# Gates and values of six batches by Strassen's scheme: seven block products in place of eight

## The chip, the core and the metric

The kernel runs on one core of one Trainium2 chip. The metric is the device time of one execution in microseconds (us); lower is better. TensorE (PE) multiplies, VectorE (DVE), ScalarE (ACT) and GpSimd (POOL) work elementwise, SyncE (SP) issues all DMAs.

## The reference, cut to what matters

```
x   = attention(q, k, v)        # 8 batches x 8 heads x 576 tokens x 64: a band of
                                # +-3 keys, plus attention over means of 4 tokens
x   = x.reshape(4608, 512)      # 8 batches x 576 tokens
out = (sigmoid(x @ w_gate) * (x @ w_val)) @ w_out    # 512 -> 1536 -> 512, all float32
```

## The kernel before

A float32 product is made of f16 products: each factor is split into a high and a low f16 part, and `product` issues three matmuls (high·high, high·low, low·high) into one accumulation. The work goes batch by batch (576 tokens, in two halves of HN = 288 columns):

- **Gates and values.** The 1536 columns of w_gate and of w_val are 12 pieces of 128 (`fc`). `moe_gate` and `moe_val` multiply one piece by the batch: 2 halves x 4 row blocks j of 128 x 3 = 24 matmuls of 128x288. ACT turns a gate into tanh, DVE forms (tanh + 1)·value (line 591), ACT writes the high f16 part of that into `gq`, DVE the low part (`split`, lines 163 and 164).
- **Output.** `moe_out` makes 4 row blocks m, each 2 halves x 12 pieces x 3 = 72 matmuls, tile `po`; ACT or DVE scales it into `osb`, SP stores it.
- **Attention.** Four units (head pairs) per batch, computed during the batch before: scores `s`, `sd`, transposes `at`, `adt`, products `x`, `od`; the tile `xs` holds a unit's x, and `xsplit` makes its f16 parts in `xT`.
- **Weights.** 36 pieces of 512 KB are loaded into four staging buffers during batch 0, unpacked from 64-bit words on ACT and DVE (`wjoin`), scaled, and split into f16 (`wsplit`: DVE, ACT, then POOL at line 251). From then on they stay in SBUF.

The order of the work is the table T: each step has a position, the steps are recorded by position, and a scheduler places the instructions of each engine in a fixed order. Each engine runs its own in that order and waits on semaphores. PSUM has 8 banks: the pool `ps_m` holds 2 tiles of 2 banks (gates, values, outputs), `ps_a` holds 4 of one bank (attention).

## Time and profile before

| what | value |
|---|---|
| median of 3 runs | 1096.45 us (1092.32 to 1097.87) |
| profiled execution | 1095.66 us, its span 1093.9 us |
| PE busy | 1063.1 us, 97% of the span |
| DVE, ACT, POOL busy | 47%, 36%, 32% |
| mean granted TensorE clock | 0.983 of full speed |

The span runs from the first to the last instruction; the execution is 1.76 us longer. PE's busy share counts a matmul from start to modelled end; how fast matmuls follow each other is read from the chain of work that ended last.

### The profile page before, as it was taken

What the parts mean: (1) busy time and instruction counts of PE and PEld (TensorE: products, weight loads), DVE (VectorE), ACT (ScalarE), POOL (GpSimd) and SP (SyncE); (2) the same over time, 40 slices, a digit from 0 to 9 for tenths busy, and PEclk for the clock granted to TensorE, in tenths of its full rate; (3) what the DMA queues carried; (4) which work ended last, traced back from release to release, by engine and by line L of the source; (5) the groups of instructions that cost most, each with busy time, mean ns of one, the idle gap of its engine ahead of it and who ended that gap; (6) DMA issues with size and microseconds to landing.
All of it is one profiled execution on the core that took longest, in us unless ns stands there. A gap on an engine that the chain in (4) does not pass through costs nothing.

```text
span 1093.9 us, 23031 instructions
## 1 busy us (share of the span) xinstructions
PE 1063.1 (97%) x9935; PEld 852.5 (78%) x9935; DVE 515.7 (47%) x1010; ACT 393.4 (36%) x878; POOL 345.5 (32%) x395
## 2 busy tenths in 40 slices
PE   9787988999999999999999999999999999999998
PEld 7575666878788787878788787878888787887776
DVE  7779989355632445234641445225452445302210
ACT  4744547233431344224341334224341344302210
POOL 7332577333321343233322333223432333100000
PEclk9779999999999999999999999999999999999999
DMA  9426643422121121221212221221112220000001
GB/s 368 154 77 212 217 177 134 138 72 74 60 83 54 63 75 59 94 82 60 97 35 93 71 75 59 83 90 53 62 46 94 82 74 1 4 32 12 1 10 36
DMA packets 33078, 91.90 MB, mean 84 GB/s; under 512 B 4688, under 2 KB 10960, under 8 KB 32976
## 3 DMA queue, kind: packets, MB, share of 16 engines
q1 hardware_dynamic: 32976, 90.42, 24.2%
q8 instruction: 78, 1.28, 0.5%
q14 instruction: 24, 0.20, 0.1%
HBM read 80.97 MB, written 9.44 MB: 83 GB/s over the span
## 4 chain that ended last, share of the span: by engine, by line
PE 86%; DVE 6%; POOL 2%; ACT 2%; DMA 2%; issue 1%; SPq 0%; ACTq 0%; DVEq 0%; POOLq 0%
PE po L365 25%; PE pg L365 23%; PE pv L365 23%; PE s L365 3%; PE x L365 3%; PE sd L365 2%; PE od L365 2%; PE at L508 1%; DMA wv<-in_wv_dram 1%; PE adt L518 1%; PE awake L82 1%; POOL wg L251 1%; DMA wg<-in_wg_dram 1%; DVE wv L209 1%; DVE hmx L159 1%
## 5 line engine op out<-in xcount | busy, mean ns | idle before, releaser
L365 PE MATMUL pg<-xT,wg 128*128 128x288 f16 x2304 | 304.7, 289 | 8.6 <-POOL wg L251 5.7
L365 PE MATMUL pv<-xT,wv 128*128 128x288 f16 x2304 | 301.8, 286 | 2.5 <-DVE tanh L591 2.4
L365 PE MATMUL po<-gq,wo 128*128 128x288 f16 x2304 | 289.4, 286 | 2.9 <-ACT wo L163 1.8
L365 PEld LDWEIGHTS <-wg 128*128 128x128 f16 x2304 | 224.5, 99 | 71.4 <-POOL wg L251 6.6
L365 PEld LDWEIGHTS <-wo 128*128 128x128 f16 x2304 | 223.3, 98 | 61.1 <-ACT wo L163 2.6
L365 PEld LDWEIGHTS <-wv 128*128 128x128 f16 x2304 | 224.0, 98 | 59.1 <-issue 3.1
L591 DVE SCALAR_TENSOR_TENSOR tanh<-tanh,pv 128x576 f32<-128x576 f32 x96 | 72.0, 750 | 203.3 <-PE pv L365 203.2
L163 ACT ACTIVATE gq<-tanh 128x576 f16<-128x576 f32 x96 | 65.6, 684 | 200.5 <-DVE tanh L591 199.8
L586 ACT ACTIVATE tanh<-pg,tsc 128x576 f32<-128x576 f32 x96 | 70.9, 739 | 123.7 <-PE pg L365 123.7
L164 DVE SCALAR_TENSOR_TENSOR gq<-tanh,gq 128x576 f16<-128x576 f32 x96 | 79.1, 824 | 25.9 <-ACT gq L163 25.4
L559 POOL TENSOR_TENSOR xT<-xs,xT 128x576 f16<-128x576 f32 x27 | 37.0, 1370 | 120.9 <-ACT xT L557 120.8
L606 DVE TENSOR_SCALAR osb<-po,osc 128x576 f32<-128x576 f32 (+1 forms) x16 | 12.8, 799 | 125.1 <-PE po L365 107.8
L442 POOL TENSOR_TENSOR t<-t,mx 128x640 f32<-128x640 f32 x32 | 41.5, 1297 | 82.6 <-DVE mx L441 81.9
L354 POOL TENSOR_TENSOR qkd<-qkd 128x576 f32<-128x576 f32 x29 | 36.2, 1249 | 93.4 <-DMA qkd<-in_qkd_dram 89.1
L430 DVE SCALAR_TENSOR_TENSOR t<-s,mk 128x384 f32<-128x384 f32 x64 | 30.0, 485 | 56.6 <-PE s L365 56.1
L608 ACT ACTIVATE osb<-po,osc 128x576 f32<-128x576 f32 (+1 forms) x17 | 12.3, 726 | 122.9 <-PE po L365 122.9
L452 POOL TENSOR_TENSOR t<-t,sm 128x640 f32<-128x640 f32 x26 | 33.7, 1296 | 57.0 <-DVE sm L450 46.3
L493 POOL TENSOR_TENSOR ad<-e,sme 72x288 f32<-72x288 f32 x50 | 32.8, 675 | 57.1 <-PE adt L518 38.4
L164 DVE SCALAR_TENSOR_TENSOR vblk<-v,svb,vblk 64x640 f16<-64x640 f32 x48 | 46.3, 965 | 5.1 <-ACT vblk L163 4.3
L365 PEld LDWEIGHTS s<-qk 64*64 64x64 f32 x1200 | 39.5, 134 | 11.0 <-issue 8.5
L448 DVE TENSOR_REDUCE sm<-t 128x10 f32<-128x640 f32 x32 | 26.1, 817 | 45.9 <-ACT t L443 45.9
L476 ACT ACTIVATE e<-sd,mxd 72x144 f32<-72x144 f32 x128 | 47.0, 370 | 2.0
(119 smaller groups left out, 1099.8 us busy)
## 6 DMA issues: line engine op xcount, KB each, us to landing
qk<-in_qk_dram SPq DMA_DIRECT2D x30, 610.0 KB, 4.3
qkd<-in_qkd_dram SPq DMA_DIRECT2D x29, 576.0 KB, 4.1
vd<-in_vd_dram SPq DMA_DIRECT2D x29, 384.0 KB, 4.6
v<-in_v_dram SPq DMA_DIRECT2D x32, 320.0 KB, 4.2
wg<-in_wg_dram SPq DMA_DIRECT2D x12, 512.0 KB, 3.6
wv<-in_wv_dram SPq DMA_DIRECT2D x12, 512.0 KB, 4.9
wo<-in_wo_dram SPq DMA_DIRECT2D x12, 512.0 KB, 3.7
out_dram<-osb SPq DMA_DIRECT2D x8, 256.0 KB, 2.1
```

The lines of the kernel that those rows point to most:

```text
L163: nc.scalar.activation(hi, src, AF.Copy, scale=sc)
L164: return nc.vector.scalar_tensor_tensor(out=lo, in0=src, scalar=sc, in1=hi, op0=ALU.mult, op1=ALU.subtract)
L354: nc.gpsimd.tensor_tensor(out=x[:, :, 0:2], in0=x[:, :, 0:2], in1=x[:, :, 2:4], op=ALU.add)
L365: nc.tensor.matmul(o, w[a], x[c], start=first and i == 0, stop=last and i == len(pairs) - 1)
L430: nc.vector.scalar_tensor_tensor(out=s["t"][:, j0:j1, :], in0=pt[:, : n * 2 * WIN].rearrange("p (a b) -> p a b", a=n), scalar=QKSCALE, in1 ...
L442: nc.gpsimd.tensor_tensor(out=t, in0=t, in1=mx.unsqueeze(2).to_broadcast([P, NBLK, WIN]), op=ALU.subtract)
L452: eng.tensor_tensor(out=t, in0=t, in1=sm.unsqueeze(2).to_broadcast([P, NBLK, WIN]), op=ALU.mult)
L476: nc.scalar.activation(s["e"][:, qb, h, :], pt[:QM, h * SD : (h + 1) * SD], AF.Exp, bias=mx[:, h : h + 1], scale=QKSCALE / 16, accum_out=s ...
L493: eng.tensor_tensor(out=AD[:, qb].rearrange("p c h k -> p h c k")[:, :, :, :KC], in0=s["e"][:, qb].rearrange("p h (c k) -> p h c k", c=NKC ...
L559: eng.tensor_tensor(out=x[:, hp, 1], in0=s["xs"], in1=x[:, hp, 0], op=ALU.subtract)
L586: nc.scalar.activation(t, pt, AF.Tanh, scale=tsc[:, b, fc : fc + 1])
L591: nc.vector.scalar_tensor_tensor(out=t, in0=t, scalar=1.0, in1=pt, op0=ALU.add, op1=ALU.mult)
```

## The change

For batches 2 to 7 two neighbouring pieces of a weight matrix (256 columns) are multiplied together, as 2x2 blocks: the rows of x (512) as two halves of two row blocks q, the weight columns as two pieces, the tokens as two halves. Strassen's scheme (Winograd's form) makes the four result blocks from seven products of sums of blocks in place of eight. Per batch there are 12 such pairs (`pair(b, n)`, gates and values alternating). A pair has seven products, each 2 x 3 = 6 matmuls of 128x288. ACT copies three of them out of PSUM into `sx`, POOL makes three sums in SBUF, DVE adds the other four from PSUM into the result tile. Then tanh, or (tanh + 1)·value and the split, run on 1152 columns at once.

- The sums of weight blocks are made once, during batch 1 (`sums(p, k)`, 12 of them). They go to HBM (`wd`) with the three plain blocks: seven blocks, 917 KB a pair. `wring` streams them back through three SBUF slots, one load per pair, 12 per batch.
- The sums of x blocks are made per two units (`xparts`).
- PSUM: `ps_m` has 5 tiles of one bank, `ps_a` 3; batches 0 and 1 keep the plain products, each half evicted by itself.
- Weights share one scale per pair of pieces; the tiles for weights, x and staging become parts of one arena, since the ring and the new tiles reuse their room. The positions in T differ.

```diff
-WGROUPS = [(0, 2), (2, 4), (4, 6), (6, 8), (8, 10), (10, NPC)]
+WGROUPS = [(0, 1), (1, 2), (2, 3), (3, 4), (4, 5), (5, 6)]
-    ps_m = ctx.enter_context(tc.tile_pool(name="ps_m", bufs=2, space=PSUM))
-    ps_a = ctx.enter_context(tc.tile_pool(name="ps_a", bufs=4, space=PSUM))
+    ps_m = ctx.enter_context(tc.tile_pool(name="ps_m", bufs=5, space=PSUM))
+    ps_a = ctx.enter_context(tc.tile_pool(name="ps_a", bufs=3, space=PSUM))
...
+        def xparts():
+            x = xq[b % 2][hp // 2]
...
+            if hp % 2 == 0:
...
+                xpair(x[:, 0:1], own[:, 0:1], nc.vector)
+                nc.gpsimd.tensor_tensor(out=tf[:, 0], in0=own[:, 1], in1=own[:, 0], op=ALU.subtract)
+                return
...
+            nc.gpsimd.tensor_tensor(out=tf[:, 1], in0=own[:, 1], in1=tf[:, 0], op=ALU.subtract)
+            nc.gpsimd.tensor_tensor(out=tf[:, 2], in0=own[:, 1], in1=even[:, 1], op=ALU.subtract)
+            xpair(x[:, 1:3], own, nc.vector)
+            nc.gpsimd.tensor_tensor(out=tf[:, 3], in0=own[:, 0], in1=tf[:, 1], op=ALU.subtract)
+            xpair(x[:, 3:7], tf, nc.vector)
...
+    def sums(p, k):
...
+        for n, (f, j) in enumerate(((0, 0), (0, 1), (1, 1))):
+            nc.sync.dma_start(wd[r][:, n], hm[:, 2 * p + f, :, :, j, :])
+        a = AST + 2 * S
+        x = place(a, 1024)
+        y = place(a + 1024, 1024)
+        nc.gpsimd.tensor_tensor(
+            out=x.rearrange("p (f c) -> p f c", f=2), in0=home[k][:, 2 * p : 2 * p + 2, 0], in1=home[k][:, 2 * p : 2 * p + 2, 1], op=ALU.add)
...
+        for d, u, w, op in ((Y[:, 0], A[:, 1, 0], A[:, 1, 1], ALU.add), (Y[:, 2], A[:, 0, 0], A[:, 1, 0], ALU.subtract),
+                            (Y[:, 1], Y[:, 0], A[:, 0, 0], ALU.subtract), (Y[:, 3], A[:, 0, 1], Y[:, 1], ALU.subtract)):
+            nc.vector.tensor_tensor(out=d, in0=u, in1=w, op=op)
+        z = x.bitcast(F16).rearrange("p (s e c) -> p s e c", s=4, e=2)
...
+        nc.scalar.copy(z[:, :, 0], y)
+        nc.vector.tensor_tensor(out=z[:, :, 1], in0=y, in1=z[:, :, 0], op=ALU.subtract)
+        nc.sync.dma_start(wd[r][:, 3:7], z.rearrange("p s e (q c) -> p s e q c", q=2))
...
+    def wring(b, n):
...
+        rg[b, n] = ring[slot[0] % NRING]
+        slot[0] += 1
+        nc.sync.dma_start(rg[b, n].rearrange("p b e q c -> p (b e q c)"), wd[n].rearrange("p b e q c -> p (b e q c)"))
+    P1, P2, P4, P3, P5, P6, P7 = (0, 0), (1, 1), (2, 6), (6, 2), (3, 3), (4, 4), (5, 5)
...
+        def go(w):
+            pt = mm(f"{name}_{w[0]}{w[1]}")
+            for q in range(2):
+                product(pt[:, :HN], [rg[b, n][:, w[0], e, q, :] for e in range(2)], [xq[b % 2][q][:, w[1], e, :] for e in range(2)], q == 0, q == 1)
+            return pt[:, :HN]
...
+            nc.scalar.copy(sx[:, 0], go(P1))
...
+            nc.scalar.copy(sx[:, 1], go(P6))
+            plus(sx[:, 1], sx[:, 1], sx[:, 0], nc.gpsimd)
...
+            nc.scalar.copy(sx[:, 2], go(P7))
+            plus(sx[:, 3], sx[:, 2], sx[:, 1], nc.gpsimd)
...
+            plus(j["c"][:, 0], go(P2), sx[:, 0])
...
+            plus(j["c"][:, 1], go(P5), sx[:, 1])
+            plus(j["c"][:, 3], j["c"][:, 1], sx[:, 2], nc.gpsimd)
...
+            plus(j["c"][:, 1], go(P3), j["c"][:, 1])
...
+            plus(j["c"][:, 2], go(P4), sx[:, 3])
```

In the order of DVE, batch 4, the second pair of pieces: before, one wide operation took a whole value tile (`pv`) from PSUM, with another for the low part behind it, and the operations of an attention unit stood between.

```order
L591 SCALAR_TENSOR_TENSOR tanh_4_2_7515<-tanh_4_2_7515,pv_4_2_7521 128x576 [waits PE_49]
L473 TENSOR_REDUCE mxd_21_0_7553<-sd_21_0_7549 72x2 [waits PE_49]
L164 SCALAR_TENSOR_TENSOR gq_112<-tanh_4_2_7515,gq_112 128x576 [waits Activation_49]
L502 TENSOR_TENSOR at16_20_7423<-at_20_3_7572,at16_20_7423 128x232 [waits Activation_49]
L591 SCALAR_TENSOR_TENSOR tanh_4_3_7606<-tanh_4_3_7606,pv_4_3_7616 128x576 [waits PE_49,Activation_49]
```

Now DVE stands in the same place as follows; `pg_4_1_11` is the product of weight block 1 and x block 1 for the gates of pair 1, and the waits on Pool are for the sums that POOL makes.

```order
L679 SCALAR_TENSOR_TENSOR tanh_112<-tanh_112,arena_109 128x1152 [waits DVE_49]
L782 TENSOR_TENSOR arena_109<-pg_4_1_11_7916,arena_109 128x288 [waits PE_49,Activation_49]
L489 TENSOR_REDUCE mx_21_7912<-t_21_7900 128x10 [waits DVE_49]
L782 TENSOR_TENSOR arena_109<-pg_4_1_33_7928,arena_109 128x288 [waits PE_49,Pool_49]
L782 TENSOR_TENSOR arena_109<-pg_4_1_26_7945,arena_109 128x288 [waits PE_49,Pool_49]
L192 SCALAR_TENSOR_TENSOR gq_111<-tanh_112,gq_111 128x2x576 [waits Activation_49]
L521 TENSOR_REDUCE mxd_21_0_7970<-sd_21_0_7966 72x2 [waits PE_49]
L782 TENSOR_TENSOR arena_109<-pg_4_1_62_7937,arena_109 128x288 [waits Pool_49]
```

DVE now empties four PSUM tiles a pair, three of them after a sum of POOL, and the operations on 1152 columns stand between them.

The second place is DVE in batch 1, where the block sums of weights (lines 742 and 746) stand between the value halves `pv_1_2` to `pv_1_4` of the plain products.

```order
L742 TENSOR_TENSOR arena_109<-arena_109 128x256 [waits Pool_49]
L742 TENSOR_TENSOR arena_109<-arena_109 128x256
L192 SCALAR_TENSOR_TENSOR vblk_129<-v9_2544,svb_139,vblk_129 64x10x64 [waits Activation_49]
L605 TENSOR_TENSOR arena_109<-xs_113,arena_109 128x288 [waits Activation_49]
L742 TENSOR_TENSOR arena_109<-arena_109 128x256 [waits DVE_49]
L679 SCALAR_TENSOR_TENSOR tanh_112<-tanh_112,pv_1_2_1_3169 128x288 [waits PE_49]
L742 TENSOR_TENSOR arena_109<-arena_109 128x256 [waits DVE_49]
L192 SCALAR_TENSOR_TENSOR gq_111<-tanh_112,gq_111 128x576 [waits Activation_49]
L746 TENSOR_TENSOR arena_109<-arena_109 128x4x256 [waits DMAHW0_49,Activation_49]
L679 SCALAR_TENSOR_TENSOR tanh_112<-tanh_112,pv_1_3_0_3230 128x288 [waits PE_49]
```

None of the rows of line 742 or 746 was there before. Each block sum starts with an addition on POOL, which waits until the store of the sum before it has left the same buffer.

The third place is SP during batch 0: stores of the plain weight blocks (`wd<-arena`) now stand ahead of weight loads, and wait for POOL's part of `wsplit`.

```order
L732 DMA wd_116<-arena_109 128x4x128 [waits DMAHW0_49,Pool_49]
L732 DMA wd_116<-arena_109 128x4x128 [waits DMAHW1_49,Pool_49]
L205 DMA arena_109<-in_wg_dram 128x1024 [waits DMAHW2_49,DVE_49]
L205 DMA arena_109<-in_wg_dram 128x1024 [waits DMAHW3_49]
L205 DMA arena_109<-in_wo_dram 128x1024 [waits DMAHW4_49,DVE_49]
```

Before, weight loads followed weight loads in this stretch of SP's queue.

## Rows read from the trace of the kernel before

**Rows 1.** The page: busy time by engine, and the chain by engine.

```profile
PE 1063.1 (97%) x9935; PEld 852.5 (78%) x9935; DVE 515.7 (47%) x1010; ACT 393.4 (36%) x878; POOL 345.5 (32%) x395
...
PE 86%; DVE 6%; POOL 2%; ACT 2%; DMA 2%; issue 1%; SPq 0%; ACTq 0%; DVEq 0%; POOLq 0%
```

**Rows 2.** Busy time in stretches: batch 0, two middle batches, the last; count in brackets.

```profile
core 0: us, PE busy (x) PEld busy (x) DVE busy (x) ACT busy (x) POOL busy (x), PEclk, DMA share, GB/s
...
90.00:120.00 30.00, 23.00 (x160) 16.50 (x159) 28.69 (x62) 15.80 (x26) 13.11 (x8) 0.90 0.65 215
120.00:150.00 30.00, 28.01 (x271) 21.18 (x269) 28.89 (x62) 15.97 (x33) 17.40 (x16) 0.98 0.62 226
...
314.20:440.60 126.40, 126.40 (x1237) 101.76 (x1234) 54.40 (x105) 42.90 (x99) 40.13 (x48) 1.00 0.22 72
440.60:567.00 126.40, 126.40 (x1237) 101.76 (x1234) 54.25 (x105) 43.02 (x99) 39.92 (x48) 1.00 0.22 72
...
946.30:1054.30 108.00, 108.00 (x915) 86.71 (x912) 22.95 (x33) 22.39 (x33) 2.96 (x2) 1.00 0.04 12
```

**Rows 3.** The chain that ended last, batch 7: start, us, what.

```profile
983.88 2.94 PE pg L365 x24
...
1051.50 2.94 PE pv L365 x24
1054.44 35.29 PE po L365 x288
```

**Rows 4.** PE's waits: for what, us in total, times, longest.

```profile
PE pg L365 <- POOL wg L251: 5.7, 3, 2.3
PE pg L365 <- ACT wg L250: 2.9, 1, 2.9
```

**Rows 5.** Groups by form: busy us, mean ns of one, then idle time before.

```profile
L591 DVE SCALAR_TENSOR_TENSOR tanh<-tanh,pv 128x576 f32<-128x576 f32 x96 | 72.0, 750 | 203.3 <-PE pv L365 203.2
L164 DVE SCALAR_TENSOR_TENSOR gq<-tanh,gq 128x576 f16<-128x576 f32 x96 | 79.1, 824 | 25.9 <-ACT gq L163 25.4
L550 DVE TENSOR_TENSOR xs<-x,od 128x464 f32<-128x464 f32 x28 | 17.8, 637 | 11.1 <-PE x L365 10.8
L550 DVE TENSOR_TENSOR xs<-x,od 128x112 f32<-128x112 f32 x28 | 7.4, 264 | 0.4 <-PE x L365 0.4
L442 POOL TENSOR_TENSOR t<-t,mx 128x640 f32<-128x640 f32 x32 | 41.5, 1297 | 82.6 <-DVE mx L441 81.9
L356 POOL TENSOR_TENSOR qks<-qkd 128x144 f32<-128x144 f32 x29 | 13.1, 451 | 90.5 <-PE sd L365 90.4
L251 POOL TENSOR_TENSOR wv<-wv 128x512 f16<-128x512 f32 x12 | 18.0, 1497 | 0.2 <-ACT wv L250 0.2
L557 ACT CAST xT<-xs 128x576 f16<-128x576 f32 x28 | 18.7, 669 | 9.0 <-DVE xs L550 7.4 <-DVE xs L548 1.3
L500 ACT CAST at<-at 128x232 f16<-128x232 f32 x24 | 8.6, 359 | 0.0
```

**Rows 6.** DMA issues: operation, count, KB each, median us from issue to landing.

```profile
qkd<-in_qkd_dram SPq DMA_DIRECT2D x29, 576.0 KB, 4.1
...
wg<-in_wg_dram SPq DMA_DIRECT2D x12, 512.0 KB, 3.6
...
out_dram<-osb SPq DMA_DIRECT2D x8, 256.0 KB, 2.1
```

**Rows 7.** The output products of batch 0: median ns, first and last start.

```profile
L365 PE MATMUL po<-gq,wo x288: 286/286/297, 173.2 to 226.5; 128*128 128x288 f16 x144
```

**Rows 8.** DVE in order of time: start, us, line, operation.

```profile
108.37 0.67 DVE L159 TENSOR_REDUCE hmx<-wv 128x1 f32<-128x512 f32 x1
108.97 0.67 DVE L159 TENSOR_REDUCE hmx<-wg 128x1 f32<-128x512 f32 x1
```

**Rows 9.** DVE's low part of gates times values: shortest, median, longest ns.

```profile
L164 DVE SCALAR_TENSOR_TENSOR gq<-tanh,gq x96: 735/759/1599, 79.6 to 1056.1; 128x576 f16<-128x576 f32 x96
```

More of the change, by code (lines that the diff above doesn't have):

```diff
@@ L81, in awake @@
         for i in range(n):
-            nc.tensor.matmul(pt[:, 0, :256], idle[:, :P], idle, start=True, stop=True)
+            nc.tensor.matmul(pt[:, :256], idle[:, :P], idle, start=True, stop=True)
     awake(30)
@@ L351, in attention_moe, with issued, pairs_done @@
     st = {}
+    xeven = {}
+    holder = {}
+    seen = set()
+    wready = set()
+    def issued(b, kinds, fcs):
+        return all((b, k, fc) in seen for k in kinds for fc in fcs)
+    def pairs_done(b):
+        return b < 2 or (b, 2 * NP - 1) in seen
     def sum4(out, x, eng=nc.gpsimd):
@@ L407, in plain_v, with bank @@
                 nc.scalar.copy(VBp[0][ps, :, ps], vraw[u][ps])
-        def bank(own, name):
-            return att(name)
+        def bank(name):
+            return mm(name) if u < NPAIR else att(name)
         def prep2():
@@ L540, in av_local @@
             if i0 == 0:
-                s["xs"] = wk.tile([P, S], F32, tag="xs", name=f"xs_{u}", bufs=1)
+                s["xs"] = xs2 if b >= 2 and u % 2 else xs1
+                assert b < 2 or all(("a", k, i) in done for k in "gvo" for i in range(NPC))
+                own(s["xs"], u)
             t0, t1 = i0 * R, min(i1 * R, S)
@@ new lines, in out_evict @@
+    def out_evict(b, m, pts):
+        osb = place(AST + 2 * S * 0 + (m % 2) * S, S) if b else stage(S)
+        assert b == 0 or all(("a", k, i) in done for k in "gvo" for i in range(NPC))
+        if m == 3:
+            seen.add((b, "out"))
+        for h, pt in enumerate(pts):
+            dst_, sc = osb[:, h * HN : (h + 1) * HN], osc[:, b : b + 1]
+            if h:
+                nc.vector.tensor_scalar(out=dst_, in0=pt[:, :HN], scalar1=sc, scalar2=None, op0=ALU.mult)
+            else:
+                nc.scalar.activation(dst_, pt[:, :HN], AF.Copy, scale=sc)
@@ L610, in moe_out @@
         for c, o, i, n in segs_of_batch(b):
             nc.sync.dma_start(out[c, m // 2][:, m % 2, o : o + n], osb[:, i : i + n])
+    MIXED = [n // 2 + NPC // 2 * (n % 2) for n in range(NFC)]
+    FIRST = {b: 0 for b in range(B)}
+    LAST = {b: MIXED[-1] if b == 0 else NFC - 1 for b in range(B)}
+    def moe_out(b, m):
+        assert all(("o", i) in done for i in range(NPC)) and issued(b, "gv", range(NFC)) and (b == 0 or (b - 1, "out") in seen)
+        pts = []
+        for h in range(2):
+            pts.append(mm(f"po_{b}_{m}_{h}"))
+            out_group(b, m, h, pts[h], MIXED if b == 0 else range(NFC))
+        out_evict(b, m, pts)
@@ L634, in at @@
             return T[f"b{u}"] + T["q" + k]
-        return T["T1"] + TB * (b - 1) + T[f"c{hp}"] + T["m" + k]
+        return start(b) + T[f"c{hp}"] * span(b - 1) / 126 + T["m" + k]
+    for i in range(6):
+        if T[f"an{i}"]:
+            add(T[f"aw{i}"], lambda n=T[f"an{i}"]: awake(n))
+    for g in ("p0", "p1", "p2", "p3", "q", "m"):
+        for chain in ("s0 s1 sm a0 a1 x", "prep2 d0 d1 dn at od x", "vd od", "v x"):
+            assert all(T[g + a] < T[g + z] for a, z in zip(chain.split(), chain.split()[1:])), (g, chain)
     known = {}
@@ L668, in attention_moe @@
     for a, e in WGROUPS:
-        p = max(JPOS[2 * a : 2 * e]) + 0.1
+        p = max(JPOS[4 * a : 4 * e]) + 0.1
         add(p, lambda a=a, e=e: wscale(a, e))
-        for i in range(a, e):
+        for i in range(2 * a, 2 * e):
             for j, k in enumerate("gv"):
```

242 lines of the change are left out of this document (186 added, 56 removed).

## The prediction

> **What bounds the kernel now.** I read the page first: PE is busy for 97% of the span and 86% of the chain that ended last is PE's [rows 1]. A busy share says little by itself, so I read stretches next: in the middle batches PE is busy in all of the 126.40 us that a batch takes, at the full granted clock (1.00, the 2.4 GHz level), while DVE, ACT and POOL have 54, 43 and 40 us of work [rows 2]. Then the chain of batch 7, which has no attention beside it: 24 groups of 24 matmuls follow each other from 983.88 to 1054.44, that is 70.56 us / 576 = 122.5 ns a matmul, and the 288 of the output take 35.29 us, 122.5 ns again [rows 3]. So a middle batch is 864 x 0.1225 = 105.8 us of gates, values and outputs and 20.6 us of attention, with nothing between. Only batch 0 is different: there DVE is busy for 28.7 and 28.9 of 30 us, PE for 23.0 and 28.0 at a clock of 0.90 and 0.98 [rows 2], and PE's waits name the weights, 5.7 us for POOL's split and 2.9 for ACT's [rows 4]. From batch 1 on PE is the bound, and matmuls taken away there come off the end, as far as the other engines keep up.
>
> **Matmuls removed: -52.9 us.** Two pieces cost 2 x 24 = 48 matmuls before; seven products of 6 cost 42. 12 pairs x 6 matmuls x 6 batches = 432, x 0.1225 = 52.9 us, 8.8 a batch: a middle batch would take 117.6 us, the last 97.0. The attention and the output products stay.
>
> **Batch 0: +3 us.** DVE is full there, so its added work moves the end. Value tiles are emptied in halves: a PSUM operation on 288 columns costs 0.45 us by the line through 264 ns for 112 columns and 637 for 464 (1.06 ns a column) [rows 5]; two of them against one of 0.75 [rows 5] is 0.15 x 12 = 1.8. Six small reductions at no more than 0.26 each (the 112-column row) are 1.6. Above, the bound is SP: in nine places a weight load now stands behind stores that wait for POOL's split, 1.5 us [rows 5], at most 13 us. Below, weights of gates and values now come ahead of more of the output's, and PE's 8.6 us of waits [rows 4] could go. I take +3 of -9 to +13, near the DVE rows, since the loads have four staging buffers in hand.
>
> **Block sums in batch 1: +4 us.** The 12 sums run one after the other through one buffer. One is: POOL on 1024 columns, from 1.95 us (line through 451 ns for 144 and 1297 for 640) to 3.0 (twice 1.50 for 512 with f16) [rows 5]; four DVE additions on 256 columns, 0.42 each, 1.7; ACT on 1024, 1.07 (0.90 ns a column from 359 and 669) [rows 5]; DVE on 1024, 1.3 (0.824 for 576 and 1.06 a column) [rows 5]; the store of 512 KB, between 2.1 (a store of 256 KB) and 3.6 (a load of 512 KB) [rows 6]. That is 8.1 to 10.7 us before any queue. The room: staging is free once batch 0's outputs are through (last matmul at 226.5 [rows 7]), and the second pair of batch 2 writes into the same room, one batch of 126.4 and some 6 us later: 132 / 12 = 11.0 a sum. The queues are not empty: the rows of DVE's order in the gate stretch of batch 1 add up to 83.6 us by the durations of rows 5 and their like, for the 85 us that PE takes there (576 x 0.1225 = 70.6, and about 14 of attention). A queue wait of 1 to 2 us a sum puts it at the edge; each 1 us over 11.0 costs 12. DVE keeps its order: what waits behind a late sum is the value halves, and behind them PE, once five banks of 1.5 us each are full. Bounds 0 and 18 (12.5 a sum); +4.
>
> **Evictions in batches 2 to 7: +8 us.** In batch 4, from the first addition to the outputs, DVE's order has 122 operations: 48 additions of 0.45, six of 1.36 and six of 1.43 on 1152 columns (0.75 and 0.824 for 576, and 1.06 a column) [rows 5], the rest attention; together 69 us. In a dense stretch operations of 0.67 start 0.60 apart [rows 8], so 0.07 x 122 comes off: 60.5. PE's time there is 504 x 0.1225 = 61.7 plus about 14 of attention (some 0.7 of its products stand there), 76. DVE is full to 80%, POOL has 34 additions of 0.70 (the same line) and attention between them. So the engines have the time; the question is order. A product is 6 x 0.1225 = 0.735 us, and product n needs the bank of n-5. P3 goes out last: after DVE has added P5 (0.45), POOL has made its sum (0.70), and DVE has come back. That leaves about 2 us before the bank is wanted again. One attention operation ahead on DVE (0.8) or POOL (1.3) fits, two in a row don't. I take 1.5 us for each of five batches and 0.5 for the last, 8; the lower bound is 0, the upper one the rival below.
>
> **What costs nothing.** A ring load is 917 KB; 256 KB land in 2.1 us and 576 KB in 4.1 [rows 6], 6.2 by that line. It is issued two pairs ahead, at least 2 x 5.1 us, and the DMA share is 0.22 [rows 2]. If SP is held for more than 4 us by another wait, PE waits for the rest. ACT's three copies (0.41 each) and 1152-column operations are some 2.7 us a pair of 5.1. The last pair's eviction, about 5.5 us, is covered by the first 60 output matmuls, 7.35 us. The end after the last matmul is as before.
>
> **Sum.** 1095.66 - 52.9 + 3 + 4 + 8 = 1057.8, say 1058 us, against the profiled execution, 0.8 below the median of the runs.
>
> **The rivals.**
> 1. *Nothing is lost.* PE stays full as before: 1095.66 - 52.9 = 1043, to 1046 with batch 0. For it: PE had no gap in the middle batches. Against: DVE's work there grows from 54 to about 74 us a batch (the 60.5 above and 14 beside the outputs).
> 2. *One of the two single stretches runs late.* Sums at 12.5 us give 14 more than forecast, 1072; SP's held loads give 10 more, 1068. For it: the sums have no second buffer.
> 3. *DVE becomes the bound of batches 2 to 6, and the kernel is slower.* An operation of a median 759 ns took up to 1599 [rows 9], 0.84 more. If all twelve wide ones of a batch do that (10.1), the overlap of starts is lost (69 us stand), and one POOL sum a pair is waited for in full (12 x 0.70 = 8.4), DVE needs 87.5 us for PE's 76: 11.5 x 5 = 57, 1043 + 7 + 57 = 1107. It decides from 76 + 52.9 / 5 = 86.6 us on. Against: the mean of that row is 824 [rows 5], so a collision is rare; half of it all gives about 1080. The Trainium skill (SBUF — State Buffer, Who interferes with whom) has a rule for this: a DVE instruction with two SBUF inputs and a GpSimd instruction that reads SBUF exclude each other for a whole instruction. By that rule the wide operations are exposed and the additions from PSUM are not, and the longest time in rows 9 agrees. By the rule with a collision each time the sum would be this rival's, by the mean of the rows it is my forecast's.
> That the products saved are not on the path is excluded by rows 2.
>
> **How the numbers follow.** Differences below 0.5%, 5.5 us, are about what a measurement of this kernel can't tell from none. My forecast, 1049 to 1067: 0.50. Rival 1, 1041 to 1049: 0.14. Rival 2, 1065 to 1080: 0.19. Rival 3 in part, 1070 to 1091: 0.07; so far that it cancels the gain: 0.04; slower: 0.06. So faster 0.90, same 0.04, slower 0.06. The range 1043 to 1080 leaves out the lowest end of rival 1 and most of rival 3, about 0.19.
>
> **What would show it.** Right: middle batches of 118 to 120 us with PE busy throughout, the last at 97; 122.5 ns a matmul; first output product of batch 0 within some us of 173; PE's waits at the end of batch 1 named by a DVE or ACT operation of the sums. Wrong: a middle batch over 123 us, DVE busy for nearly all of it (rival 3); waits on the ring's loads; PE idle long enough that the granted clock falls below 1.00 in middle batches, where its matmuls would take longer too.

## The result: 1.2% faster, a third of the forecast gain

The changed kernel takes 1082.68 us (median of 4 runs, 1082.34 to 1082.9) against 1096.3 us: the ratio of the times is 0.988, with a 95% interval of 0.9855 to 0.9907. The forecast was 1058 us, with a range of 1043 to 1080.

The page of the changed kernel, busy time by engine and the chain by engine (answers to [rows 1]):

```profile
PE 1025.9 (95%) x9511; PEld 810.3 (75%) x9511; DVE 744.7 (69%) x1366; ACT 488.1 (45%) x1089; POOL 610.7 (57%) x647
...
PE 58%; DVE 19%; POOL 9%; issue 5%; ACT 5%; DMA 3%; SPq 0%; POOLq 0%; DVEq 0%; ACTq 0%
```

PE has 424 matmuls fewer on record, but its share of the chain has fallen from 86% to 58%. Where the time went is read from the output products, whose first and last start mark the batches (answers to [rows 7]); here batches 0, 1, 2, 3, 4 and 7:

```profile
L413 PE MATMUL po<-gq,wo x288: 284/286/448, 164.8 to 217.2; 128*128 128x288 f16 x144
L413 PE MATMUL po<-gq,wo x288: 282/286/296, 315.0 to 356.1; 128*128 128x288 f16 x144
L413 PE MATMUL po<-gq,wo x288: 283/286/296, 440.3 to 480.7; 128*128 128x288 f16 x144
L413 PE MATMUL po<-gq,wo x288: 284/286/296, 565.1 to 605.4; 128*128 128x288 f16 x144
L413 PE MATMUL po<-gq,wo x288: 284/286/296, 689.8 to 730.2; 128*128 128x288 f16 x144
L413 PE MATMUL po<-gq,wo x288: 286/286/287, 1041.3 to 1076.5; 128*128 128x288 f16 x144
```

Set against [rows 2, 7], in the terms of the forecast:

| part | forecast | measured |
|---|---|---|
| batch 0, to its last output product (226.5 before) | +3 | 217.2 - 226.5 = -9.3 |
| batch 1, gates and values (314.2 - 226.5 = 87.7 before) | +4 | (315.0 - 217.2) - 87.7 = +10.1 |
| batches 2 to 6, from outputs to outputs | 5 x (-8.8 + 1.5) = -36.5 | (940.9 - 315.0) - 5 x 126.4 = -6.1 |
| batch 7 | -8.8 + 0.5 = -8.3 | (1041.3 - 940.9) - 108.0 = -7.6 |

(940.9 is the first output product of batch 6.) The four misses are -12.3, +6.1, +30.4 and +0.7, together 24.9 us. Batch 7, which has no attention beside it, gained nearly what the scheme promises. The five middle batches should have taken about 119 us and take 125.2 in the mean. Batch 0's figure comes from one execution of each kernel. In the experiments below that keep the order of the changed kernel, batch 0 ends anywhere from 214.5 to 221.9 us, so the 9.3 is good to some 5 us.

PE's visible waits in the pairs of batch 4 come to 3.7 us, and all three name DVE (for what, us in total, times, longest):

```profile
PE pg L413 <- DVE arena L782: 1.7, 2, 1.0
PE sd L413 <- DVE t L478: 1.2, 1, 1.2
PE at L556 <- DVE at L550: 0.8, 1, 0.8
```

In the windows of the same batch they lie in the last 20 us (columns as in [rows 2]; the fourth row is the pairs as a whole):

```profile
565.10:605.00 39.90, 39.90 (x405) 32.61 (x403) 17.77 (x32) 11.03 (x21) 13.15 (x16) 1.00 0.33 111
605.00:670.00 65.00, 64.89 (x615) 50.00 (x615) 48.07 (x92) 35.20 (x81) 50.71 (x57) 1.00 0.59 202
670.00:689.80 19.80, 16.06 (x149) 12.40 (x148) 19.73 (x26) 10.01 (x26) 14.19 (x16) 1.00 0.37 130
605.40:689.80 84.40, 80.55 (x755) 62.08 (x753) 67.80 (x117) 45.21 (x106) 64.90 (x72) 1.00 0.54 186
...
979.30:1041.30 62.00, 62.00 (x508) 49.39 (x505) 34.69 (x57) 26.22 (x47) 33.19 (x35) 1.00 0.40 138
```

In those last 20 us DVE is busy for 19.73 of 19.80 us; over all the pairs it is busy for 67.80 of 84.40. What it is busy with shows in order of time, DVE first, then POOL (start, us, line, operation):

```profile
668.68 0.81 DVE L600 TENSOR_TENSOR arena<-x,od 128x464 f32<-128x464 f32 x2
669.67 4.90 DVE L192 SCALAR_TENSOR_TENSOR vblk<-v,svb,vblk 64x640 f16<-64x640 f32 x1 [0.17 <-ACT vblk L191]
674.49 0.44 DVE L782 TENSOR_TENSOR arena<-pv,arena 128x288 f32<-128x288 f32 x1
```

```profile
669.73 0.79 POOL L782 TENSOR_TENSOR arena<-arena 128x288 f32<-128x288 f32 x1
670.48 0.80 POOL L625 TENSOR_TENSOR arena<-arena 128x288 f32<-128x288 f32 x1
671.23 0.80 POOL L626 TENSOR_TENSOR arena<-arena,xs 128x288 f32<-128x288 f32 x1
671.98 1.16 POOL L402 TENSOR_TENSOR qkd<-qkd 128x576 f32<-128x576 f32 x1
673.08 0.80 POOL L782 TENSOR_TENSOR arena<-arena 128x288 f32<-128x288 f32 x1
673.83 1.39 POOL L628 TENSOR_TENSOR arena<-arena 128x288 f32<-128x288 f32 x1
```

The operation on 64x640 makes the low f16 part of the attention's values (`vblk`). It reads two tiles in SBUF and takes 0.87 us at the least. Here it takes 4.90, and it ends in the first operation of POOL that runs longer than its like (1.39 for 0.80), after five that run back to back. Over the whole kernel (shortest, median, longest ns; then busy us and the mean, 1583 ns):

```profile
L192 DVE SCALAR_TENSOR_TENSOR vblk<-v,svb,vblk x48: 868/1127/4900, 229.4 to 957.7; 64x640 f16<-64x640 f32 x48
```

```profile
L192 DVE SCALAR_TENSOR_TENSOR vblk<-v,svb,vblk 64x640 f16<-64x640 f32 x48 | 76.0, 1583 | 4.2 <-ACT vblk L191 3.4
```

Batch 1 has the same picture. Two additions of block sums (line 742, 0.42 us each in the median) take 3.53 us on DVE beside a row of POOL's; the value halves are evicted behind them, and PE waits 2.66 us, and 4.37 at another such place:

```profile
257.06 3.53 DVE L742 TENSOR_TENSOR arena<-arena 128x256 f32<-128x256 f32 x2 [1.60 <-POOL arena L736]
```

```profile
263.56 1.25 PE L413 MATMUL pg<-arena 128*128 128x288 f16 x8 [2.66 <-DVE tanh L679]
...
301.56 0.55 PE L556 MATMUL at<-ident,t 128*128 128x128 f32 x3 [4.37 <-DVE t L478]
```

These waits are 7.0 of batch 1's 10.1 us. The rest goes with the clock: up to the first wait the granted clock is 1.00, behind it 0.93 in the mean, and as many matmuls (432) keep PE busy for 46.86 us in place of 43.70:

```profile
217.20:263.50 46.30, 43.70 (x432) 34.82 (x430) 39.61 (x70) 20.33 (x49) 22.72 (x21) 1.00 0.36 123
263.50:315.00 51.50, 46.86 (x432) 36.05 (x432) 44.58 (x72) 23.67 (x51) 25.23 (x22) 0.93 0.32 110
```

### The profile page after: what moved, and what is told of

The parts are those of the page before. It is cut to its first block, busy times and chain, and to the rows that moved or that the text cites. A ratio compares the mean times of both kernels' runs of the same rounds, so it can differ in the third digit from the quotient of the medians.

```text
span 1080.4 us, 23529 instructions
## 1 busy us (share of the span) xinstructions
PE 1025.9 (95%) x9511; PEld 810.3 (75%) x9511; DVE 744.7 (69%) x1366; ACT 488.1 (45%) x1089; POOL 610.7 (57%) x647
## 4 chain that ended last, share of the span: by engine, by line
PE 58%; DVE 19%; POOL 9%; issue 5%; ACT 5%; DMA 3%; SPq 0%; POOLq 0%; DVEq 0%; ACTq 0%
PE po L413 26%; PE pg L413 11%; PE pv L413 10%; POOL arena L782 4%; PE x L413 3%; PE s L413 2%; PE od L413 2%; POOL t L490 2%; DVE vm L187 1%; PE sd L413 1%; DVE arena L782 1%; DMA qkd<-in_qkd_dram 1%; DVE arena L742 1%; DVE tanh L679 1%; DVE gq L192 1%
## 5 line engine op out<-in xcount | busy, mean ns | idle before, releaser
L413 PEld LDWEIGHTS <-arena 128*128 128x128 f16 x4176 | 404.7, 98 | 129.5 <-issue 13.9
L413 PE MATMUL pg<-arena 128*128 128x288 f16 x2088 | 282.4, 290 | 12.2 <-DVE arena L782 5.2
L413 PE MATMUL pv<-arena 128*128 128x288 f16 x2088 | 281.8, 287 | 2.0 <-DVE arena L782 0.6
L782 POOL TENSOR_TENSOR arena<-arena 128x288 f32<-128x288 f32 x198 | 195.5, 995 | 67.8 <-ACT arena L792 52.4
L782 DVE TENSOR_TENSOR arena<-pv,arena 128x288 f32<-128x288 f32 x144 | 62.6, 444 | 59.1 <-POOL arena L782 49.2
L192 DVE SCALAR_TENSOR_TENSOR vblk<-v,svb,vblk 64x640 f16<-64x640 f32 x48 | 76.0, 1583 | 4.2 <-ACT vblk L191 3.4
L191 ACT ACTIVATE gq<-tanh 128x576 f16<-128x576 f32 (+1 forms) x42 | 37.4, 890 | 62.6 <-DVE tanh L679 62.6
L192 DVE SCALAR_TENSOR_TENSOR gq<-tanh,gq 128x576 f16<-128x576 f32 (+1 forms) x42 | 52.8, 1256 | 4.0 <-ACT gq L191 4.0
L413 PE MATMUL s<-qk 64*64 64x64 f32 x1200 | 54.4, 227 | 0.0
L413 PE MATMUL sd<-kdblk,qks 128*72 128x288 f32 x128 | 43.2, 420 | 10.3 <-DVE t L478 6.1
L191 ACT ACTIVATE vblk<-v,svb 64x640 f16<-64x640 f32 x48 | 39.6, 825 | 12.3 <-DVE svb L184 6.0
```

The costliest lines, as they stand in the source:

```text
L191: nc.scalar.activation(hi, src, AF.Copy, scale=sc)
L192: return nc.vector.scalar_tensor_tensor(out=lo, in0=src, scalar=sc, in1=hi, op0=ALU.mult, op1=ALU.subtract)
L413: nc.tensor.matmul(o, w[a], x[c], start=first and i == 0, stop=last and i == len(pairs) - 1)
L782: eng.tensor_tensor(out=dst_, in0=x, in1=y, op=ALU.add)
```

## The experiments

Four theories of the middle batches: **1**, a DVE operation with two SBUF inputs and a POOL operation exclude each other; **2**, the turn DVE, POOL, DVE within a pair is too long; **3**, DVE simply has too much to do; **4**, PE itself loses time where attention is cut into small pieces. "A middle batch" below is batch 4, from its first output product back to that of batch 3, in the profiled execution; the changed kernel has 124.8 us there, and 125.2 in the mean of batches 2 to 6. The mean is given where it tells something else.

**Work that nobody waits for.** Two DVE operations more in each pair of batch 7, on a tile of their own, with two SBUF inputs or with one.

```diff
+            dummy()      # in s7 and in s5, b == 7 only
+nc.vector.tensor_tensor(out=d[:, :S], in0=d[:, :S], in1=d[:, S:], op=ALU.add)   # dummy_two
+nc.vector.tensor_reduce(d[:, :1], d[:, S:], axis=AX.X, op=ALU.max)              # dummy_one
```

> Theory 1 (exclusion): in the middle batches a DVE operation with two SBUF inputs and a POOL operation hold each other up, and that lengthens the pairs of products. Theory 2 (turns): what is lost is the wait of P5 and P3 for sums that go from DVE to POOL and back, whatever the operations' inputs. Theory 3 (load): DVE has too much to do where attention is dense, whatever the kind. Batch 7 has no attention, and its 12 pairs take 61.9 us, PE's own time. Here each of these pairs gets two DVE additions on 576 columns with both inputs in SBUF, on a buffer of their own that nobody waits for: 24 operations of about 0.7, 16 to 17 us, which takes DVE from 34.7 to about 51 of 62 us, near the 67.8 of 84.8 us in the dense stretch of batch 4. Theory 1: POOL's sums of 288 columns go from a mean of 0.97 us to 1.05 or more, the additions themselves to 0.85 or more, and the pairs take 63.5 to 68. Theories 2 and 3: the additions take about 0.7, the pairs 62 to 64, and the same as with operations of one input. Whole kernel: +1 to +6 by theory 1, 0 to +2 by the others.

> The same as the run with two inputs, with 24 maxima over 576 columns with one SBUF input in place of the additions (about 0.7 us each by the 810 ns of one over 640). Theory 1: POOL's sums stay at a mean of 0.97 us, the maxima at 0.7, the pairs at 62 to 62.5. Theories 2 and 3: pairs as long as with two inputs, within 0.5 us. If both runs leave the pairs at 62, load and exclusion without the attention's own order cost nothing, and theory 2 or the dense places of attention remain.

Ratios 0.991 (0.9876 to 0.9945) and 0.9893 (0.9866 to 0.9921). The edit missed its aim: nothing held the operations in batch 7, and the scheduler ran all of them in batch 6, 8 beside its pairs and 16 beside its outputs. So the pairs of batch 7 stayed at 62.0 us in both, those of batch 6 grew from 85.3 to 88.7 and 88.3, and neither expectation was put to the test. One thing can be read all the same, the durations (shortest, median, longest ns):

```profile
L828 DVE TENSOR_TENSOR dum<-dum x24: 744/758/1801, 917.3 to 963.3; 128x576 f32<-128x576 f32 x24
```

```profile
L828 DVE TENSOR_REDUCE dum<-dum x24: 736/744/753, 924.6 to 969.6; 128x1 f32<-128x576 f32 x24
```

With one input none of these operations is stretched, with two some are. The 8 in the pairs of batch 6 are 7.9 us of DVE's time with two inputs and 6.0 with one, and the pairs grew by 3.4 and 3.0 us: added work cost something there, whatever its kind, though the scheduler moved other operations as well.

**Work moved to another engine.** `sums_on_dve` takes POOL's three sums of a pair to DVE, `v_off_dve` the values' low part from DVE to POOL.

```diff
-            plus(sx[:, 1], sx[:, 1], sx[:, 0], nc.gpsimd)
+            plus(sx[:, 1], sx[:, 1], sx[:, 0])
...
-                split(VB[ps, 0, :, ps], VB[ps, 1, :, ps], vraw[u][ps], svb[ps, b : b + 1])
+                nc.scalar.activation(vraw[u][ps], vraw[u][ps], AF.Copy, scale=svb[ps, b : b + 1])
+                nc.scalar.copy(VB[ps, 0, :, ps], vraw[u][ps])
+                nc.gpsimd.tensor_tensor(out=VB[ps, 1, :, ps], in0=vraw[u][ps], in1=VB[ps, 0, :, ps], op=ALU.subtract)
```

> POOL's three sums of a pair (36 a batch, 288 columns) go to DVE. The output is the reference's. No turn DVE, POOL, DVE is left in a pair, and POOL has only the attention's work; DVE gets 36 operations of about 0.45, 16 us a batch, and its stretched operations shrink (the values' split from 1.6 to about 0.9 us: 5.6 us a batch; the wide ones on 1152 columns by 0.1 to 0.2 each). Theory 1: middle batches 120 to 123, 11 to 25 us faster than the change. Theory 2: 118.5 to 121, 20 to 33 faster. Theory 3: DVE goes from 85 to about 95 of 118 us, in the dense stretch from 68 to about 75 of 76: 125 to 130, 0 to +25.

> The split of the attention's values (two DVE operations of two SBUF inputs on 64x640 per unit, 0.87 us at the least and up to 4.90, mean 2.12 in the dense stretch of batch 4) is taken from DVE: ACT scales in place, ACT makes the high part, POOL subtracts. The output is the reference's. Theory 1: 8 operations a batch leave DVE, with 8 x about 1.6 us, and POOL gets 8 x 1.3, which no DVE operation then loses its turn to; the middle batches go from 125.2 to 121 to 123, the kernel 11 to 20 us faster than the change. Theory 2: no turn of the products gets shorter, and POOL has 10 us a batch more: 125 to 128, 0 to +14. Theory 3 (DVE's load): DVE has 13 us a batch less, 122 to 124, so 6 to 16 faster. The scheduler moves other instructions too.

Both are slower than the change: 0.9978 (0.996 to 0.9996) and 0.9957 (0.9944 to 0.9971). Batches 2 to 6 take 125.2 to 129.6 us in `sums_on_dve`; in `v_off_dve` batch 2 takes 137.1 and the others 125.2 to 125.6. The windows of batch 4's pairs, first `sums_on_dve`, then `v_off_dve`:

```profile
611.70:700.20 88.50, 83.73 (x756) 64.34 (x755) 80.10 (x156) 45.02 (x106) 34.45 (x40) 0.96 0.50 177
```

```profile
614.70:702.10 87.40, 84.53 (x795) 64.88 (x793) 60.58 (x117) 51.77 (x118) 77.22 (x82) 1.00 0.52 180
```

One fills DVE (80.1 of 88.5 us), the other POOL (77.2 of 87.4). By what was written before, theory 1 fails in both: the first falls to theory 3, the second to theory 2. But the scheduler reorders all engines after such an edit, and these two runs don't say which of load and order counts. From here on the order is held: the order that the scheduler finds for the changed kernel is read out, and each engine's instructions are chained in it.

```diff
+        for a, b in zip(names, names[1:]):      # names: one engine's instructions, in the order of the change
+            tc.add_manual_dep(have[b], a, mybir.DependencyInfo(mybir.DependencyClass.NoSync, mybir.DependencyReason.DATA), reason="order")
```

**One SBUF input in place of two, nothing else moved.** These kernels and `small_pool_sums` leave parts of the result out; they are there to be timed. In their traces DVE, ACT and POOL run the same operations in the order of the change, one for one.

```diff
+        if one and not PLAIN[0]:                # the values alone; then all of batches 1 to 7
+            return nc.vector.tensor_reduce(lo[..., 0], hi, axis=AX.X, op=ALU.max)
         return nc.vector.scalar_tensor_tensor(out=lo, in0=src, scalar=sc, in1=hi, op0=ALU.mult, op1=ALU.subtract)
...
+            n = HN if PLAIN[0] or eng is nc.vector or b == 2 else 16      # small_pool_sums
+            eng.tensor_tensor(out=dst_[:, :n], in0=x[:, :n], in1=y[:, :n], op=ALU.add)
```

> Every engine's instructions stand in exactly the order of the changed kernel (the scheduler's order of it is read out and pinned). One thing differs: the 48 DVE operations that make the low part of the attention's values read one SBUF input in place of two (a maximum over the same 64x640, of about the same bare time, 0.8 against 0.87 us). The low part is left out of the result by that. Theory 1 (exclusion): they take 0.8 each where they took 1.58 in the mean and up to 4.90; the wait of 3.7 us in the last third of a middle batch goes for the most part; middle batches 121 to 122.5, the kernel 10 to 20 us faster than the change. Theory 2 (turns DVE, POOL, DVE) and theory 3 (too much to do for DVE at bare durations): the order and the bare load are the same, so within 3 us of the change.

> The same pinned order. Besides the values' low parts, DVE's other operations with two SBUF inputs in batches 1 to 7 read one: the block sums of batch 1, the product of gates and values, the low parts of it and of the blocks of x, each as a maximum or copy over as many columns. The output is not the reference's. Theory 1: no DVE operation waits out a row of POOL's; both waits of batch 1 go (2.7 and 4.4 us, and some 3 that the lower clock after them costs), its gate stretch goes from 97.8 to 88 to 91; middle batches 120 to 122 (what stays is PE's own loss by attention in small pieces, some 4 us a batch); the kernel 20 to 35 us faster than the change, 1048 to 1063. Theories 2 and 3: 1076 to 1085.

> The same pinned order. POOL's three sums of a pair, in batches 3 to 7, are made on 16 columns of 288 (so the output is not the reference's): each takes some 0.2 us instead of 0.8 to 1.0, which shortens the turn DVE, POOL, DVE and takes 20 us a batch from POOL. Theory 2: the turns are what is lost, so batches 3 to 6 come to 120 to 121. Theory 1: fewer operations stand in POOL's rows, but the long ones of attention still do; 121 to 123. Theory 3 (DVE's bare load): 124 to 125. The kernel: 15 to 20 faster by theory 2, 8 to 16 by theory 1, 0 to 4 by theory 3.

| run | us | ratio | middle batch | mean of batches 2 to 6 | gates and values of batch 1 |
|---|---|---|---|---|---|
| the change | 1082.68 | 0.9881 (0.9855 to 0.9907) | 124.8 | 125.2 | 97.8 |
| one_input_values | 1062.94 | 0.9695 (0.9663 to 0.9726) | 120.7 | 121.6 | 93.9 |
| one_input_all | 1050.26 | 0.9555 (0.9513 to 0.9598) | 119.8 | 120.1 | 87.1 |
| small_pool_sums | 1064.27 | 0.9706 (0.9666 to 0.9745) | 120.9 | 122.2 (its batch 2 has whole sums) | 98.0 |

The values' operations now take this (shortest, median, longest ns, `one_input_values`):

```profile
L212 DVE TENSOR_REDUCE vblk<-vblk x48: 805/821/826, 232.7 to 937.9; 64x10 f16<-64x640 f16 x48
```

And batch 1 and batch 4 in windows, `one_input_all`:

```profile
221.90:309.00 87.10, 86.83 (x863) 69.43 (x861) 70.86 (x139) 43.78 (x99) 41.67 (x42) 1.00 0.39 130
590.40:669.90 79.50, 79.50 (x756) 62.18 (x755) 57.90 (x117) 45.24 (x106) 53.48 (x72) 1.00 0.58 197
```

The order and the bare load are the change's own, and PE waits for nothing in the pairs; in the change the same stretch, 605.40 to 689.80, had DVE at 67.80 and POOL at 64.90. So exclusion added 9.9 us of DVE's time and 11.4 of POOL's to the pairs of batch 4, and cost 124.8 - 119.8 = 5.0 us of a middle batch (5.1 in the mean) and all of batch 1's 10.1 and a little more. Theories 2 and 3 expected no gain from this and fall as accounts of their own. What theory 2 blames, DVE's wait for POOL's sums, did not even change with the values' operations (batch 4, first the change, then `one_input_values`):

```profile
DVE arena L782 <- POOL arena L782: 4.6, 7, 1.4
DVE arena L803 <- POOL arena L803: 4.7, 6, 1.9
```

`small_pool_sums` alone would have misled: its 120.9 us, and its 18 us off the change, are what was written for theory 2 (120 to 121, 15 to 20), and just beyond theory 1's (121 to 123, 8 to 16). It shortens the turns, but it also takes away POOL's time beside which DVE is kept out, so it can't tell the two apart.

The operations put in here write less than those they replace, and are of another kind. That this is not what counts shows in the change itself: its additions from PSUM (line 782, `TENSOR_TENSOR` on 288 columns, one input in SBUF) are never stretched, at 384 to 459 ns in 288 operations on `pg` and `pv`. But not each DVE operation with one SBUF input is free. A small `TENSOR_SCALAR` of attention goes from 0.15 to 0.82 us:

```profile
L531 DVE TENSOR_SCALAR sme<-sme x32: 152/168/823, 15.8 to 937.7; 72x4 f32<-72x4 f32 x32
```

In batch 4 one starts at 632.58 and takes 0.77 us, as long as POOL's addition beside it (632.54, 0.79). So two SBUF inputs are not the only form that is exposed here.

**Attention in whole groups.** In the change the scheduler cuts the local scores into pieces between products; PE's timeline:

```profile
614.32 0.33 PE L413 MATMUL s<-qk 64*64 64x64 f32 x4
614.59 2.38 PE L413 MATMUL pv<-arena 128*128 128x288 f16 x18
...
669.82 1.15 PE L413 MATMUL s<-qk 64*64 64x64 f32 x32
670.90 1.64 PE L413 MATMUL pv<-arena 128*128 128x288 f16 x12
```

Four matmuls hold PE for 0.27 us (614.32 to 614.59), 32 for 1.08: 0.034 each in a long piece, so 0.13 of the 0.27 is a border. The edit puts each group where its first piece stood.

```diff
+        if ref.startswith("s_") and int(ref.split("_")[1]) >= 8:
+            if ref not in groups:
+                groups[ref] = []
+                keep.append(groups[ref])
+            groups[ref] += loads + [n]
```

> The same pinned order but for PE: the local scores of attention in batches 2 to 7 (64x64 matmuls in groups of 24 and 16, which the scheduler cuts into 2 to 4 pieces between products) stand together, each group where its first piece stood. The output is the reference's. Theory 4: a piece costs PE 0.16 us at its borders (6.95 us in 14 pieces after, 5.66 in 6 before, for the same 160 matmuls), so 1.0 to 1.3 us a batch come off, 5 to 7 us in all. If instead the products behind a whole group come late for the other engines, 0 or slower.

> The run with one input for all (119.8 us a middle batch; the low parts, the products and the block sums are left out of the result) with the scores in whole groups as well. If exclusion (5.0 us a batch) and pieces of attention (1.8 to 2.4) are all that is lost, a middle batch comes to 117.4 to 118.2, PE's own 117.6, and the kernel to 1038 to 1045. If both removed the same wait, 119 to 120 and 1047 to 1052.

`scores_whole`: 1077.9 us, ratio 0.9824 (0.9797 to 0.985), a middle batch 122.4, which is 2.4 less where 1.0 to 1.3 were expected; in the mean of batches 2 to 6 it is 1.6 less (123.6), and the profiled execution, 1073.1 us, was the fastest of its five. `one_input_all_whole`: 1038.54 us, 0.9484 (0.9439 to 0.953), a middle batch 118.2, in the mean 118.6. Theory 4 holds, beside theory 1: 5.0 for exclusion, 1.6 for pieces on top of it, and 0.6 is left over PE's 117.6. The borders alone were priced at 1.0 to 1.3 of that 1.6; what the rest is, no run separates.

**POOL made to wait.** If DVE loses its turn to a whole row, a wait on POOL behind DVE's operation should give most of it back, with nothing left out. First at the places that the scheduler's order gives, then at the 49 places where the trace of the change has a stretched operation.

```diff
+    for dve, pool in waits:
+        dep(dve, pool, mybir.DependencyClass.Sync)
```

> The changed kernel with every engine's order pinned and nothing left out; the output is the reference's. Added are waits: behind each DVE operation that makes the low part of the values, the POOL operation that the scheduler puts next waits until that operation is through. Theory 1 in its sharper form (DVE loses its turn to each next operation of a row on POOL, not to one alone): the values' operations wait for one POOL operation at most, 1.0 to 1.2 us in the mean (1.58 before, the longest 4.90), the longest under 2.3; middle batches 121.5 to 123.5; the kernel 6 to 16 us faster than the change. If one POOL operation's time were all that DVE loses, or if POOL's sums come as much later as DVE is earlier: 0 to +5.

> The same for each DVE operation with two SBUF inputs in the whole program (POOL's next operation waits for it), and with the local scores of attention in whole groups, as in the run scores_whole. The output is the reference's. Theory 1: the gate stretch of batch 1 goes from 97.8 to 89 to 93, middle batches from 122.4 (whole groups alone) to 118.5 to 121, the kernel to 1048 to 1065. If POOL becomes late by its waits (some 100 of them, up to 1.4 us each): middle batches stay at 122 or grow, 1075 or more.

> The changed kernel with every engine's order pinned; the output is the reference's. In the trace of the changed kernel 49 DVE operations with two SBUF inputs, from batch 1 on, took over 0.25 us more than the shortest of their form, 52.7 us more in all. Here, for each of them, the POOL operation that began next in that trace waits until the DVE operation is through. If DVE loses its turn to each operation of a row on POOL: the values' operations at 1.0 us in the mean and under 2.5 at the longest; batch 1's gate stretch 90 to 94, middle batches 121 to 123, the kernel 10 to 20 us faster than the change. If one POOL operation's time is lost either way: as the change, within 4 us.

> The same with the local scores of attention in whole groups. The output is the reference's. If both add up (12 to 20 and 5 to 12): middle batches 119 to 121, the kernel 1055 to 1068. If the shift of PE's order moves the collisions away from the places of the waits: 1070 to 1078, no better than whole groups alone.

Ratios 0.9847 (0.9801 to 0.9893), 0.9902 (0.9872 to 0.9933), 0.9873 (0.984 to 0.9907) and 0.9816 (0.9786 to 0.9847), middle batches of 123.8, 123.9, 123.7 and 123.1. The values' operations do get shorter (first row), and so does DVE's busy time in batch 4's pairs, from 67.80 to 61.89 (second row), but DVE's wait for POOL's sums, 4.6 us in the change, is 8.5 (third row), all of `waits_on_chip`:

```profile
L225 DVE SCALAR_TENSOR_TENSOR vblk<-v,svb,vblk x48: 868/1050/2907, 230.9 to 955.0; 64x640 f16<-64x640 f32 x48
```

```profile
605.50:688.90 83.40, 80.52 (x756) 62.28 (x755) 61.89 (x121) 45.62 (x106) 65.29 (x73) 1.00 0.55 188
```

```profile
DVE arena L815 <- POOL arena L815: 8.5, 9, 2.5
```

The pairs get 1.0 us shorter for these 5.9 (0.7 in the mean of batches 2 to 6). My expectation was wrong: POOL now stands back, and most of the time that DVE no longer loses comes back as its wait for POOL's sums. What costs is that the two can't run together, more than who goes first. With whole groups the waits at the 49 places add nothing that can be measured (0.9816 for 0.9824), and those behind every operation with two SBUF inputs make the kernel slower (0.9902).

**Values read from PSUM.** ACT puts the scaled values into PSUM, so that DVE's operation has one SBUF input and nothing is left out.

```diff
-                split(VB[ps, 0, :, ps], VB[ps, 1, :, ps], vraw[u][ps], svb[ps, b : b + 1])
+                nc.scalar.activation(VB[ps, 0, :, ps], vraw[u][ps], AF.Copy, scale=svb[ps, b : b + 1])
...
+                nc.scalar.activation(pt, vraw[u][:, g].rearrange("p a b -> p (a b)"), AF.Copy, scale=svb[:, b : b + 1])
+                for ps in HALVES:
+                    nc.vector.tensor_tensor(out=VB[ps, 1, g, ps], in0=pt[ps].rearrange("p (a b) -> p a b", b=D), in1=VB[ps, 0, g, ps], op=ALU.subtract)
```

> The low part of the attention's values is made by DVE from a scaled copy that ACT puts into PSUM (two operations of 128x320 on ACT more a unit, four of 64x320 on DVE in place of two of 64x640), so DVE's operations read one SBUF input. The output is the reference's. The scheduler's order is not pinned. Theory 1: no such operation over 0.55 us, 2.2 us a unit or less in place of 3.2 in the mean; middle batches 121 to 123, the kernel 1062 to 1073. If the new order, or two banks of three that the copies hold, costs as much: 124 to 127, 1080 to 1095.

> The same with the local scores of attention in whole groups, the order otherwise pinned to that of values_from_psum. The output is the reference's. 5 to 10 us below values_from_psum, as in scores_whole; 1055 to 1066 if theory 1 carries it.

1084.83 us, 0.9903 (0.9866 to 0.994), and 1083.02 us, 0.9898 (0.986 to 0.9937); middle batches of 126.2 and 125.6. The operations did what they should (421/489/495 ns: a `TENSOR_TENSOR` with one input in PSUM, none of 96 stretched). But the order is a new one. It loses most in batch 2 (133.9 us for 125.3, in several waits of up to 2.6 us), and in batch 4 it has a place where POOL is the one kept out, DVE first, then POOL:

```profile
680.00 1.34 DVE L685 SCALAR_TENSOR_TENSOR tanh<-tanh,arena 128x1152 f32<-128x1152 f32 x1
681.26 0.45 DVE L527 TENSOR_REDUCE mxd<-sd 72x2 f32<-72x288 f32 x1
681.63 1.34 DVE L611 TENSOR_TENSOR arena<-arena 128x1152 f16<-128x1152 f32 x1
...
683.69 1.35 DVE L192 SCALAR_TENSOR_TENSOR gq<-tanh,gq 128x1152 f16<-128x1152 f32 x1
687.45 0.46 DVE L788 TENSOR_TENSOR arena<-pg,arena 128x288 f32<-128x288 f32 x1 [2.42 <-POOL arena L788]
```

```profile
679.94 5.39 POOL L404 TENSOR_TENSOR kdblk<-qkd 64x144 f32<-64x144 f32 x2
685.41 1.26 POOL L490 TENSOR_TENSOR t<-t,mx 128x640 f32<-128x640 f32 x1
```

Two POOL operations with a median of 0.44 us take 5.39 while DVE runs its wide ones; then DVE waits 2.42 for POOL, and PE 3.18 for DVE. So the run bears out the operations' part of theory 1; the kernel's time, 1062 to 1073 by it, missed, and the new order hides what the shorter operations are worth.

**Batch 0.** Its gain of 9.3 us was not in the forecast. Three runs: the kernel before with batch 0's new places in the table; the change with batch 0's attention on its own three banks; the kernel before with that attention, but for its transposes, on the products' banks. The order is not held in any of them.

```diff
-            return mm(name) if u < NPAIR else att(name)     # attention_banks, in the change
+            return att(name)
...
-            return att(name)                                # before_more_banks, in the kernel before
+            return mm(name)[:, 0] if u < NPAIR else att(name)
```

> The kernel before the change with only those numbers of the table taken over that place batch 0's attention, weight conversions and their engines (te2 and te3 from DVE to POOL among them). If batch 0's gain of 9.3 us comes from these places: gates start at 58 to 61 us instead of 66.7, batch 0's outputs end at 217 to 221 instead of 226.5, the kernel 6 to 10 us faster than before. If it comes from the banks or the weights' loads of the changed kernel: within 2 us of before.

> The changed kernel, but batch 0's attention takes its PSUM banks from the three of attention alone, not from the five of the products (empty then). The output is the reference's. If batch 0's gain comes from these banks: gates start at 63 to 72 us instead of 58.9 and batch 0's outputs end at 222 to 232 instead of 217.2. If not: within 2 us of the change there.

> The kernel before the change, but batch 0's attention takes its banks from the two double tiles of the products (empty then) for all but its transposes. The output is the reference's. If batch 0's gain comes from banks: gates start at 59 to 63 us instead of 66.7. If it needs the new places as well, or comes from elsewhere: 65 to 68.

`attention_banks` takes 1093.45 us, ratio 0.9968 (0.9944 to 0.9992). Gates begin at 58.9 us in the change (first row) and at 67.0 in `attention_banks` (second row), and batch 0's outputs end at 226.7:

```profile
L413 PE MATMUL pg<-arena x288: 282/286/448, 58.9 to 150.7; 128*128 128x288 f16 x144
```

```profile
L413 PE MATMUL pg<-arena x288: 286/286/448, 67.0 to 166.7; 128*128 128x288 f16 x144
```

So without the five banks, in the order that the scheduler then makes, the change's gain in batch 0 is gone. It is not in the places alone: `before_new_places` takes 1107.18 us (1.0115, 1.0063 to 1.0167), with gates from 66.8 us. And banks alone don't help the kernel before: `before_more_banks` takes 1107.44 us (1.0102, 1.0065 to 1.014), with gates from 78.1. In both, batch 0 ends near 237 us and the other batches take what they took before. `attention_banks` came out as written for the banks; the other two were expected to be within some us of the kernel before or faster, and why they are slower stays open.

## Why the prediction was wrong, step by step

- **Matmuls removed** was right for the products: the pairs of batch 7 take 62.00 us for the 70.56 of [rows 3], 8.6 of the 8.8 forecast, and with exclusion and pieces gone a middle batch takes 118.2 us for the 117.6 worked out. Its last sentence, that attention stays, was not: in pieces attention costs 1.6 to 2.4 us a batch more.
- **"Evictions in batches 2 to 7: +8"** is the step that failed. It put 1.5 us on each of five batches; measured are 125.2 - 117.6 = 7.6, of which exclusion is 5.0. The bare sum was right: DVE forecast at 60.5 us for 76 of PE, measured at 57.90 in `one_input_all`. Over the whole stretch the engines do have the time, even with the collisions (67.80 of 84.40 us). What failed is the overlap: "One attention operation ahead on DVE (0.8) or POOL (1.3) fits" in the 2 us of slack takes the durations of the kernel before as fixed. In the change one operation of 0.87 us took 4.90, DVE was full for the last 20 us of the pairs, and PE waited 3.7 there.
- The exclusion was there as rival 3, but it was priced by the mean in rows 9, from a kernel whose POOL is busy for 32% of the span and whose wide operations are few, and at 0.84 us at most for one collision. With POOL at 57% and DVE at 69% the collisions cost 5.0 us in each of five batches, 25 in all. Most of DVE's 9.9 us is on operations that the rival didn't count: the six on the values in batch 4 take 2.12 us each in the mean, 7.5 us in all over their 0.87. Rival 3 in part had 1070 to 1091 and 7 in 100, and the time fell there. But its "about 1080" halves the result, 57 us, and not the causes: half of 10.1, 8.5 and 8.4 leaves DVE at 74 us for PE's 76, and nothing would have been lost by the rival's own rule. The Trainium skill (SBUF — State Buffer, Who interferes with whom) has the rule that speaks against the change: a DVE instruction with two SBUF inputs contends with a GpSimd instruction that reads SBUF, and one with at most one SBUF input does not, outside what the page calls 2-port modes. The runs agree: with two SBUF inputs an operation of 0.87 us took up to 4.90, the maxima with one took 0.83 at most, and with the second input in PSUM 0.50. Whether the stretched `TENSOR_SCALAR` was in a 2-port mode, no run shows.
- **"Block sums in batch 1: +4"** was too small by 6 us, and for another reason than it named: the single buffer and the store don't bind, since without exclusion the stretch takes 87.1 us, before's 87.7. The lower clock behind PE's waits, some 3 of the 10.1 us, was not in the sum.
- **"Batch 0: +3"** missed an edit of one line, the banks that batch 0's attention may use; what its terms would have been worth, no run shows. This is luck: without that line, which takes no product away, the change gains 0.3% (`attention_banks`). The forecast was 25 us too low: 37 us too low for the other batches, and 12 too high here.
- **What costs nothing** held: no wait of PE in the middle batches names a ring load, which lands in 4.7 us in the median (6.2 forecast). Of the signs, a middle batch over 123 us came true; DVE busy for nearly all of it and a clock below 1.00 there did not.

The version with whole score groups, at 0.9824, leaves nothing out and is faster than the kernel before; over the change it gains about half a percent, and the two intervals (0.9797 to 0.985 and 0.9855 to 0.9907) lie just apart.
